# Two heads in one product, quads of heads, and four fixed PSUM areas in a fused attention and expert kernel

## The chip, the cores and the metric

The kernel runs on one core of a Trainium2 chip. The metric is the device time of one execution in microseconds (us); for the kernel before it is the median of three runs. The core has five engines with queues of their own: PE (TensorE, matrix products; its weight loads are shown as PEld), DVE (VectorE), ACT (ScalarE), POOL (GpSimd) and SP (SyncE). PE writes to PSUM; ACT and DVE read PSUM. Each engine takes its instructions in order, and an instruction that waits for another engine holds up all that is queued behind it.

## The reference

Sliding-window causal attention (window 64) over 8 batches, 8 heads, 576 positions and head size 64, then a soft mixture of experts whose slots are fed by a softmax over all 4608 tokens:

```python
scores = scale * np.matmul(q, k.transpose(0, 1, 3, 2))      # q, k, v: 8 x 8 x 576 x 64
rel = pos[:, None] - pos[None, :]
scores = np.where((rel >= 0) & (rel < 64), scores, -1e9)
attn = softmax(scores, axis=-1)
x = np.matmul(attn, v)                                      # then 4608 tokens x 512
logits = x @ phi                                            # 512 x 32 slots
slot_input = softmax(logits, axis=0).T @ x                  # over tokens; 8 experts x 4 slots x 512
slot_out[e] = np.maximum(slot_input[e] @ w1[e], 0) @ w2[e]  # 512 -> 1024 -> 512
out = softmax(logits, axis=1) @ slot_out                    # 4608 x 512
```

## The kernel before

The order of the work is written out by hand. A pair is two heads of one batch: 32 pairs, four to a batch. A loop over n = 0 to 39 (a step) runs a pipeline of stages on different pairs; each step works on one pair in each stage.

- st_transpose(n), L232: 36 transposes of 64x64 on PE bring the pair's queries and keys (tiles qs and ks, loaded as fp16) into a PSUM tile tp with the head size on the partitions. st_copy(n), L235 on ACT, copies them to SBUF, to qkT, one of four.
- st_max(n-1): products of 32 queries by 96 keys on top of a mask, L243 (the mask, 2 x 480 columns) and L250 (36 small products); DVE takes each row's maximum, L253.
- st_shift(n-2): a product L258 turns the maxima round, and DVE copies them, L262, into rt, one of three, from which a product subtracts them before exp.
- st_score(n-3): products with the mask and shift (L270, L274: 8 of 128 columns) and the scores themselves (L278, L283: 64 keys by 64 queries, each head on its half of the partitions). st_exp: exp on ACT, L291 for the last block, L292 for the eight others, into pt.
- st_av(n-4): attention times V, 20 products (L305, L307), with V in two layouts, one shifted by 64 rows by POOL (shift_v, L158 and L159). st_norm on DVE: reciprocal L316 and scaling L317, into x_b.
- fr_transpose(n-5): x_b transposed on PE (L331), copied by ACT (L332) into xt.

Once in a batch, each in a step of its own, come the front stages: logits and their online softmax over tokens (fr_logits at n = 4b+9, L339; fr_exp, L345 to L361), the dispatch transposes (n = 4b+10, L386 to L392) with the softmax over slots (fr_combine, L371 to L382), and the slot sums (n = 4b+11, L399 and L402, accumulated by DVE at L411).

All PSUM tiles of this loop come from one pool of four buffers that go round, whatever the name:

```python
psum = patt.enter_context(tc.tile_pool(name="psum", bufs=4, space=bass.MemoryType.PSUM))
def banks(name):
    t = psum.tile([128, 2, 512], FP32, name=name, tag="ps")
```

Inside a step the stages are called in this order: transposes, scores, copy, exp, attention times V, shift, norm, maxima, logits, x transposes, the rest of the front stages. Loads of q, k and v are made for a whole batch on POOL's queue, the expert weights one tensor every third step; the last expert's weights go into the buffers of q and k after step 32.

After the loop comes the tail, a chain on small data: merging the softmax statistics (L492 to L526), experts 0 to 3 as a group of four in the columns of PE (ha L541, tht L551, op L557), experts 4 to 7 one after the other (hp_ps L570, ReLU on ACT L573, so_ps L578), then the output (cp L595, copies L600 and L602 and the output DMAs).

Of the kernel before, what the change touches and what calls it, by code (L numbers as in the profile page):

```python
# [14 lines left out]
NEG = -60000.0  # L15
# [3 lines left out]
def kernel(  # L19
# [32 lines left out]
    psum = patt.enter_context(tc.tile_pool(name="psum", bufs=4, space=bass.MemoryType.PSUM))  # L52
    pin = ctx.enter_context(tc.tile_pool(name="pin", bufs=2))

    def banks(name):
        t = psum.tile([128, 2, 512], FP32, name=name, tag="ps")
        return t, t[:, :, :].bitcast(FP16)
# [4 lines left out]

    def flat(src, b):
        return src[b].rearrange("h s d -> (h s) d").rearrange("(c p) d -> p c d", p=128)

    def rows(src, b):
        return src[b].rearrange("h s d -> (h s d)").rearrange("(g p x) -> p g x", p=128, x=RQ * Dh)

    staged = {}

    def new_qk(b):
        staged[b] = tuple(pin.tile([128, HP, RQ * Dh], FP16, name=n, tag=n) for n in ("qs", "ks"))

    def load_qk(b, c0=0, c1=HP):
        for t_, src in zip(staged[b], (q, k)):
            nc.gpsimd.dma_start(out=t_[:, c0:c1, :], in_=rows(src, b)[:, c0:c1, :])

    new_qk(0)
    load_qk(0, 0, 1)

    ident_h = const.tile([128, 128], FP16, name="ident_h")
    make_identity(nc, ident_h)
    load_qk(0, 1, HP)
# [22 lines left out]
    def load_last():  # L106
        e = E - 1
        w1_t[e], w2_t[e] = [], []
        for i in range(2):
            a = pin.tile([128, 2, F], FP16, name="w1h", tag="qs")  # L110
            nc.gpsimd.dma_start(out=a, in_=w1_dram(e)[:, 2 * i:2 * i + 2, :])
            w1_t[e].extend(a[:, j, :] for j in range(2))
        for i in range(2):
            c = pin.tile([128, 4, D], FP16, name="w2h", tag="ks")
            for j0, j1 in ((0, 4),) if i == 0 else ((0, 2), (2, 4)):
                nc.gpsimd.dma_start(out=c[:, j0:j1, :], in_=w2_dram(e)[:, 4 * i + j0:4 * i + j1, :])
            w2_t[e].extend(c[:, j, :] for j in range(4))


    wb = const.tile([32, 96], FP16, name="wb")  # L120
    nc.vector.memset(wb, 0.0)
    nc.gpsimd.affine_select(out=wb, in_=wb, compare_op=ALU.is_gt, fill=NEG,
                            base=0, pattern=[[1, 96]], channel_multiplier=-1)
    nc.gpsimd.affine_select(out=wb, in_=wb, compare_op=ALU.is_ge, fill=NEG,
                            base=64, pattern=[[-1, 96]], channel_multiplier=1)

    KR = 75
    mb = const.tile([64, 128], FP16, name="mb")
    nc.vector.memset(mb, 0.0)
    nc.gpsimd.affine_select(out=mb[:, 0:64], in_=mb[:, 0:64], compare_op=ALU.is_gt,  # L130
                            fill=NEG, base=0, pattern=[[1, 64]], channel_multiplier=-1)
    nc.gpsimd.affine_select(out=mb[:, 64:128], in_=mb[:, 64:128], compare_op=ALU.is_ge,
                            fill=NEG, base=0, pattern=[[-1, 64]], channel_multiplier=1)
    db = const.tile([128, 12], FP16, name="db")
    nc.vector.memset(db[64:128, :], 0.0)
    nc.gpsimd.affine_select(out=db[64:KR, 0:10], in_=db[64:KR, 0:10], compare_op=ALU.not_equal, fill=-1.0,
                            base=0, pattern=[[-1, 10]], channel_multiplier=1)
    nc.gpsimd.affine_select(out=db[64:KR, 10:11], in_=db[64:KR, 10:11], compare_op=ALU.not_equal, fill=NEG,
                            base=-10, pattern=[[0, 1]], channel_multiplier=1)
    nc.gpsimd.affine_select(out=db[64:KR, 11:12], in_=db[64:KR, 11:12], compare_op=ALU.not_equal, fill=1.0,  # L140
                            base=-10, pattern=[[0, 1]], channel_multiplier=1)
# [9 lines left out]
    v2s = [pvv.tile([128, NCH, VP], FP16, name=f"v2_{i}") for i in range(2)]  # L151

    def load_v(b):
        nc.gpsimd.dma_start(out=v1s[b % 2][:, :, 0:Dh], in_=flat(v, b))  # L154

    def shift_v(b):
        v1, v2 = v1s[b % 2], v2s[b % 2]
        nc.gpsimd.tensor_copy(out=v2[64:128, :, 0:Dh], in_=v1[0:64, :, 0:Dh])  # L158
        nc.gpsimd.tensor_copy(out=v2[0:64, 1:NCH, 0:Dh], in_=v1[64:128, 0:NCH - 1, 0:Dh])  # L159

    load_v(0)
    new_qk(1)
    load_qk(1)

    NQ = 4
    qkT = [pqk.tile([128, 2, 64 + S], FP16, name=f"qkT{i}") for i in range(NQ)]
    for t_ in qkT:
        nc.vector.memset(t_[:, 1, 0:64], 0.0)
    wm = const.tile([128, 5, 96], FP16, name="wm")
    for t in range(4):  # L170
        nc.vector.tensor_copy(out=wm[32 * t:32 * t + 32],
                              in_=wb[:, :].unsqueeze(1).broadcast_to([32, 5, 96]))
    nc.vector.memset(wm[0:32, 0, 0:64], NEG)
    nc.vector.memset(wm[32:64, 0, 0:32], NEG)

    lh = const.tile([128, 10, 128], FP16, name="lh")
    nc.vector.tensor_copy(out=lh[0:64], in_=mb[:, :].unsqueeze(1).broadcast_to([64, 10, 128]))
    nc.vector.tensor_copy(out=lh[64:128], in_=db[64:128, 0:10].unsqueeze(2).broadcast_to([64, 10, 128]))
    for u in (0, 5):
        nc.vector.tensor_tensor(out=lh[64:128, u, 0:64], in0=lh[64:128, u, 0:64],  # L180
                                in1=db[64:128, 10:11].broadcast_to([64, 64]), op=ALU.add)
    NR = 3
    rts = [const.tile([128, 128], FP16, name=f"rt{i}") for i in range(NR)]
    for rt in rts:
        nc.vector.memset(rt[64:128, 64:128], 0.0)
        nc.vector.tensor_copy(out=rt[64:128, 0:64], in_=db[64:128, 11:12].broadcast_to([64, 64]))
        nc.vector.tensor_copy(out=rt[0:64, 0:64], in_=ident_h[0:64, 0:64])
        nc.vector.tensor_copy(out=rt[0:64, 64:128], in_=ident_h[0:64, 0:64])
# [37 lines left out]
    def st_transpose(p, tq):  # L226
        b, hp = divmod(p, HP)
        for w, src in enumerate(staged[b]):
            for r in range(RQ):
                for hl in range(2):  # L230
                    h = slice(64 * hl, 64 * hl + 64)
                    nc.tensor.transpose(tq[h, w, 64 * r:64 * r + 64], src[h, hp, Dh * r:Dh * r + Dh], ident_h[h, h])  # L232

    def st_copy(p, tq):
        nc.scalar.activation(qkT[p % NQ][:, :, 64:64 + S].rearrange("p w (g r) -> p w g r", r=RQ),  # L235
                             tq[:, :, 0:S].rearrange("p w (r g) -> p w g r", r=RQ), AF.Copy, scale=QKS)

    def st_max(p):
        qk = qkT[p % NQ]
        m = pw.tile([128, 10], FP16, name="m", tag="m")  # L240
        mx, _ = banks("mx")
        for hl in range(2):
            nc.tensor.matmul(mx[:, hl, 0:480], ident_h[:, :], wm[:, :, :].rearrange("p c x -> p (c x)"),  # L243
                             start=True, stop=False, skip_group_check=True)
        for c in range(5):
            for t in range(4 if c < 4 else 2):
# [10 lines left out]
    def st_shift(p, av):  # L257
        nc.tensor.matmul(av[64:74, 1, 384:512], mts.pop(p)[:, :], ident_h[:, :], start=True, stop=True,  # L258
                         skip_group_check=True)
# [380 lines left out]
```

## Time and profile before

| | |
|---|---|
| median of the runs | 270.45 us (269.38 to 273.96, three runs) |
| the profiled execution | 271.76 us, of which the program's span is 270.0 us |
| granted PE clock, mean over the span | 0.799 |
| attention stage: first copy L235 / last copy L235 start | 6.03 / 179.19 us |
| tail: first step of the chain / last copy of the output | 207.2 / 255.5 us |
| HBM read, written | 61.93 MB, 9.44 MB |

In the profile the span is cut into 40 equal slices, in which a digit is the busy share of an engine in tenths; PEclk is the granted share of PE's full clock. A line of a group of instructions gives source line, engine, operation, output<-input, shapes and count, then the busy time of all and the mean ns of one, then the engine's idle time just ahead of them and what ended most of it. A timeline line gives start, duration, engine, line and operation; several equal instructions in a row are merged (x18), with the time from the first's start to the last's end.

### The profile page before, as it was taken

How to read it: one execution, taken by the hardware profiler on the slowest of the kernel's cores; microseconds unless marked ns; L12 is line 12 of the kernel's file. 1: busy time of each engine (PE TensorE's matmuls, PEld its weight loads, DVE VectorE, ACT ScalarE, POOL GpSimd, SP SyncE). 2: the span in 40 equal slices, each digit the busy share in tenths (PEclk: the TensorE clock that was granted, in tenths of full speed). 3: DMA queues.
4: the chain of work that ended last, by engine and by line, in shares of the span. 5: the costliest groups of instructions: out<-in, count | busy, mean ns of one | idle time of the engine just before them, and what ended most of it. 6: DMA issues, size and time to landing. Idle time of an engine off the chain costs nothing. (4 is left out here: it accounts for less than half of the span.)

```text
span 270.0 us, 9905 instructions
## 1 busy us (share of the span) xinstructions
PE 185.6 (69%) x4563; PEld 122.6 (45%) x4563; DVE 140.9 (52%) x313; ACT 120.5 (45%) x215; POOL 78.0 (29%) x74
## 2 busy tenths in 40 slices
PE   2386858858868897887887586878663488866400
PEld 1254646646646665665665365555531134521100
DVE  2743563674754576674485554656664621056510
ACT  2235445655455475574654647462632111155400
POOL 8566064342370533443057033740000000000000
PEclk9998989986985897997799689975955557995555
DMA  6999997992999599199299959899960000029996
GB/s 84 175 206 210 181 208 131 177 207 38 132 211 208 58 187 206 17 177 208 37 100 210 210 73 184 121 203 205 210 105 0 0 4 0 2 101 344 359 359 234
DMA packets 63625, 41.06 MB, mean 152 GB/s; under 512 B 38496, under 2 KB 54880, under 8 KB 63584
## 3 DMA queue, kind: packets, MB, share of 16 engines
q0 software_dynamic: 58064, 30.94, 84.3%
q1 hardware_dynamic: 5520, 9.50, 10.2%
q8 instruction: 35, 0.57, 0.8%
q14 instruction: 6, 0.05, 0.1%
HBM read 61.93 MB, written 9.44 MB: 264 GB/s over the span
## 5 line engine op out<-in xcount | busy, mean ns | idle before, releaser
L235 ACT ACTIVATE qkT<-tp 128x1152 f16<-128x1152 f16 x32 | 36.2, 1131 | 50.2 <-PE tp L278 39.6
L253 DVE TENSOR_REDUCE m<-mx 128x10 f16<-128x960 f32 x32 | 36.8, 1150 | 6.4 <-PE mx L250 6.2
L262 DVE CAST rt<-av 10x128 f16<-10x128 f32 x32 | 9.2, 289 | 51.6 <-PE av L258 50.9
L292 ACT ACTIVATE pt<-sc 128x1024 f16<-128x1024 f32 x32 | 32.9, 1029 | 0.6 <-PE sc L283 0.5
L332 ACT COPY xt<-f 128x576 f16<-128x576 f16 x32 | 20.5, 640 | 26.5 <-PE f L331 26.5
L154 POOL DMA_DIRECT2D v<-in_v_dram x8 | 14.6, 1823 | 55.3 <-issue 35.2
L158 POOL COPY v<-v 64x2304 f16<-64x2304 f16 x8 | 16.8, 2102 | 41.6 <-DMA v<-in_v_dram 41.6
L317 DVE TENSOR_TENSOR x_b<-av,rc 128x640 f16<-128x640 f32 x32 | 26.4, 824 | 1.1
L305 PE MATMUL av<-v,pt 128*64 128x65 f16 x576 | 19.7, 214 | 8.0 <-issue 8.0
L232 PE MATMUL tp<-ident_h,qs 64*64 64x64 f16 x576 | 17.6, 210 | 11.0 <-DMA qs<-in_q_dram 7.9
L274 PE MATMUL sc<-rt,lh 128*128 128x128 f16 x256 | 23.9, 247 | 1.4 <-issue 1.4
L243 PE MATMUL mx<-wm,ident_h 128*128 128x480 f16 x64 | 21.7, 426 | 3.0 <-ACT pt L291 2.7
L305 PEld LDWEIGHTS <-pt 128*64 128x64 f16 x576 | 15.3, 125 | 12.2 <-issue 8.6
L232 PEld LDWEIGHTS <-qs 64*64 64x64 f16 x576 | 14.2, 122 | 14.4 <-DMA qs<-in_q_dram 8.0
L232 PE MATMUL tp<-ident_h,ks 64*64 64x64 f16 x576 | 17.6, 210 | 4.6 <-issue 2.4
L250 PEld LDWEIGHTS <-qkT 64*32 64x32 f16 x1152 | 11.3, 97 | 18.5 <-issue 18.3
L274 PEld LDWEIGHTS <-lh 128*128 128x128 f16 x256 | 18.4, 113 | 1.6 <-issue 1.6
L283 PE MATMUL sc<-qkT 64*128 64x64 f16 x512 | 15.8, 205 | 4.4 <-issue 4.4
L331 PE MATMUL f<-ident_h,x_b 128*128 128x128 f16 x160 | 16.3, 240 | 2.5 <-ACT pt L291 1.2
L250 PE MATMUL mx<-qkT 64*32 64x96 f16 x1152 | 16.2, 221 | 2.2 <-issue 2.2
L232 PEld LDWEIGHTS <-ks 64*64 64x64 f16 x576 | 14.6, 125 | 5.1 <-DMA ks<-in_k_dram 2.6
L159 POOL COPY v<-v 64x2240 f16<-64x2240 f16 x8 | 16.4, 2052 | 0.5
(135 smaller groups left out, 295.0 us busy)
## 6 DMA issues: line engine op xcount, KB each, us to landing
w<-in_moe_w_dram POOLq DMA_DIRECT2D x14, 1024.0 KB, 15.6
out_dram<-ob SPq DMA_DIRECT2D x16, 512.0 KB, 4.5
v<-in_v_dram POOLq DMA_DIRECT2D x8, 576.0 KB, 8.4
qs<-in_q_dram POOLq DMA_DIRECT2D x7, 576.0 KB, 9.6
ks<-in_k_dram POOLq DMA_DIRECT2D x7, 576.0 KB, 11.6
w1h<-in_moe_w_dram POOLq DMA_DIRECT2D x2, 512.0 KB, 18.6
out_dram<-ob SPq DMA_DIRECT2D x8, 128.0 KB, 4.5
w2h<-in_moe_w_dram POOLq DMA_DIRECT2D x1, 512.0 KB, 19.1
```

Of the source, the lines that this page charges most:

```text
L158: nc.gpsimd.tensor_copy(out=v2[64:128, :, 0:Dh], in_=v1[0:64, :, 0:Dh])
L159: nc.gpsimd.tensor_copy(out=v2[0:64, 1:NCH, 0:Dh], in_=v1[64:128, 0:NCH - 1, 0:Dh])
L232: nc.tensor.transpose(tq[h, w, 64 * r:64 * r + 64], src[h, hp, Dh * r:Dh * r + Dh], ident_h[h, h])
L235: nc.scalar.activation(qkT[p % NQ][:, :, 64:64 + S].rearrange("p w (g r) -> p w g r", r=RQ), tq[:, :, 0:S].rearrange("p w (r g) -> p w g r ...
L243: nc.tensor.matmul(mx[:, hl, 0:480], ident_h[:, :], wm[:, :, :].rearrange("p c x -> p (c x)"), start=True, stop=False, skip_group_check=True)
L250: nc.tensor.matmul(mx[32 * t:32 * t + 32, hl, 96 * c:96 * c + 96], qk[r, 0, 64 + o:64 + o + 32], qk[r, 1, o:o + 96], start=False, stop=Tru ...
L253: nc.vector.reduce_max(m[:, :].rearrange("p (l c) -> p l c", l=2), mx[:, :, 0:480].rearrange("p l (c x) -> p l c x", x=96), axis=AXX)
L274: nc.tensor.matmul(sc[:, hl, 128 * c:128 * c + 128], lh[:, 5 * hl + c, :], rt[:, :], start=(c == 0), stop=False, skip_group_check=True)
L292: nc.scalar.activation(pt[:, :, 0:8, :].rearrange("p l i x -> p l (i x)"), sc[:, :, :], AF.Exp, scale=XS)
L305: nc.tensor.matmul(av[r0:r0 + 64, hl, 65 * (i // 2):65 * (i // 2) + 65], pt[:, hl, i, :], rhs, start=True, stop=True, skip_group_check=True)
L317: nc.vector.tensor_tensor(out=xbs[b][:, :, 128 * hp:128 * hp + 128].rearrange("p c (l d) -> p l c d", l=2), in0=avv[:, :, :, 0:64], in1=rc ...
L332: nc.scalar.copy(out=xts[b][:, hp, :], in_=fq[:, 0, 0:S])
```

## The change

- Four fixed PSUM areas a_t, a_v, a_m and a_s, of two banks each, take the place of the pool. a_t takes the transposes of q or k and the last (ninth) block of scores; a_v takes the ninth block of the maxima, the turned maxima and attention times V; a_m takes the other eight blocks of the maxima, and then all of the front stages (x transposes, logits, dispatch, slot sums); a_s takes eight blocks of scores.
- Loads and transposes are by quads: four heads of q or of k, half a batch. An even step transposes a quad's keys, an odd one its queries, 18 transposes each of 128x64. The keys are copied by ACT to kT with two heads on each pair's 128 partitions; the queries by two ACT instructions to qb, in which each block of 128 columns has one head's 64 queries in the upper half of the partitions and the other's in the lower, and zeros elsewhere. A pair is now heads i and i+2 of a quad.
- With that, one product over all 128 partitions gives the scores of two heads: maxima are 9 products of 128x128 on the mask, scores 9 of 128x128 on mask and shift.
- The order in a step is: transposes and their copy, shift and its copy, maxima, attention times V and norm, scores and exp, front stages. The maxima run two steps behind the transposes (one before), the shift three (two before), so only two rt buffers stand.
- x transposes are made for two pairs at once in every second step. fr_exp first copies the logits from PSUM to SBUF on ACT.
- Loads: one DMA for each quad of k, q and v, and the V shift by half batches.
- Tail: experts 0 to 3 and 4 to 6 as two groups in the columns of PE, expert 7 alone as before; so4 is copied by DVE alone.

```diff
-    psum = patt.enter_context(tc.tile_pool(name="psum", bufs=4, space=bass.MemoryType.PSUM))
+    psum = patt.enter_context(tc.tile_pool(name="psum", bufs=1, space=bass.MemoryType.PSUM))
...
+    a_t, a_v, a_m, a_s = [psum.tile([128, 2, 512], FP32, name=n_) for n_ in ("a_t", "a_v", "a_m", "a_s")]
+    a_th, a_mh = a_t[:, :, :].bitcast(FP16), a_m[:, :, :].bitcast(FP16)
...
+    def st_transpose(n, tq):
+        g, odd = divmod(n, 2)
+        src = staged.pop(("qs" if odd else "ks", g))
+        tf = tq.rearrange("p a x -> p (a x)")
+        for r in range(RQ):
+            for hf in range(2):
+                nc.tensor.transpose(tf[64 * hf:64 * hf + 64, 128 * r:128 * r + 128],
+                                    src[:, hf, Dh * r:Dh * r + Dh], ident_h[:, :])
+
+    def st_copy(n, tq):
...
+        if odd:
+            for hf in range(2):
+                h = slice(64 * hf, 64 * hf + 64)
+                nc.scalar.activation(qbs[g % 2][h, :, :, hf, :], tf[h], AF.Copy, scale=QKS)
+        else:
+            nc.scalar.activation(kTs[g % NK][:, :, 64:64 + S], tf, AF.Copy, scale=QKS)
...
     def st_max(p):
...
+        mx = a_m
+        m8 = a_v[:, 0, 384:512]
+        nc.tensor.matmul(m8, ident_h[:, :], wm[:, 1, :], start=True, stop=False, skip_group_check=True)
+        nc.tensor.matmul(m8, qblock(p, 8), kwindow(p, 8), start=False, stop=True, skip_group_check=True)
+        for j in range(2):
+            nc.tensor.matmul(mx[:, j, :], ident_h[:, :], wm[:, j:j + 4, :].rearrange("p c x -> p (c x)"),
                              start=True, stop=False, skip_group_check=True)
...
+        for i in range(8):
+            nc.tensor.matmul(at(mx, m8, i), qblock(p, i), kwindow(p, i), start=False, stop=True,
+                             skip_group_check=True)
+        nc.vector.reduce_max(m[:, 8:9], m8, axis=AXX)
+        nc.vector.reduce_max(m[:, 0:8].rearrange("p (l c) -> p l c", l=2),
+                             mx[:, :, :].rearrange("p l (c x) -> p l c x", x=128), axis=AXX)
...
+    def st_shift(p):
+        t_ = a_v[64:64 + NB, 1, 384:512]
+        nc.tensor.matmul(t_, mts.pop(p)[:, 0:NB], ident_h[:, :], start=True, stop=True, skip_group_check=True)
+        nc.vector.tensor_copy(out=rts[p % NR][64:64 + NB, :], in_=t_)
...
+        sc, sm = a_s, a_t[:, 1, 128:256]
+        for order in (range(8), (8,)):
+            for i in order:
+                nc.tensor.matmul(at(sc, sm, i), lh[:, i, :], rt[:, :], start=(i % 4 == 0), stop=False,
+                                 skip_group_check=True)
+            for i in order:
+                nc.tensor.matmul(at(sc, sm, i), kwindow(p, i), qblock(p, i), start=False, stop=True,
+                                 skip_group_check=True)
+        nc.scalar.activation(pt[:, 0:8, :].rearrange("p i x -> p (i x)"), sc[:, :, :], AF.Exp, scale=XS)
+        nc.scalar.activation(pt[:, 8, :], sm, AF.Exp, scale=XS)
...
     def fr_exp(b, lg):
+        lg_ps, lg = lg, pw.tile([128, 192], FP32, name="lg", tag="lgec")
+        nc.scalar.copy(out=lg, in_=lg_ps)
...
+        f, fq = a_m, a_mh
         if n < NP:
+            st_transpose(n, a_th)
+            st_copy(n, a_th)
         if 0 <= n - 3 < NP:
+            st_shift(n - 3)
+        if 0 <= n - 2 < NP:
+            st_max(n - 2)
         if 0 <= n - 4 < NP:
+            st_av(n - 4, a_v)
+            st_norm(n - 4, a_v)
+        if 0 <= n - 3 < NP:
+            st_score(n - 3)
...
+        xp = n - 6 if n % 2 == 0 and 0 <= n - 6 < NP else None
...
+    groups = ((0, 1, 2, 3), (4, 5, 6))
...
+    for g, es in enumerate(groups):
+        ha, _ = banks("ha")
...
+            if f2 == 0:
+                nc.scalar.activation(hs[g][0:n, 0:512], ha[0:n, 0, :], AF.Relu, scale=emask[0:n, g:g + 1])
+            else:
+                nc.vector.tensor_scalar(out=hs[g][0:n, 512:1024], in0=ha[0:n, 1, :], scalar1=emask[0:n, g:g + 1],
+                                        scalar2=0.0, op0=ALU.mult, op1=ALU.max)
...
-    so4 = ptl.tile([128, D], FP16, name="so4")
-    nc.scalar.copy(out=so4[:, 0:256], in_=so_ps[:, 0:256])
-    nc.vector.tensor_copy(out=so4[:, 256:512], in_=so_ps[:, 256:512])
+    so4 = ptl.tile([128, D], FP16, name="so4")
+    nc.vector.tensor_copy(out=so4, in_=so_ps)
```

The prediction names lines of the new kernel too: L241 its transposes, L250 and L252 the copies of queries and keys, L267 the first product of the maxima's ninth block, L276 the maximum on DVE, L283 DVE's copy of the shift, L296 and L297 the two exps, L339 the x transposes.

## The prediction

> **What bounds the kernel now.** I read the page first, for the engines' shares and the clock.
>
> ```profile
> PE 185.6 (69%) x4563; PEld 122.6 (45%) x4563; DVE 140.9 (52%) x313; ACT 120.5 (45%) x215; POOL 78.0 (29%) x74
> ...
> PE   2386858858868897887887586878663488866400
> ...
> PEclk9998989986985897997799689975955557995555
> ```
>
> ```profile
> L235 ACT ACTIVATE qkT<-tp 128x1152 f16<-128x1152 f16 x32 | 36.2, 1131 | 50.2 <-PE tp L278 39.6
> L253 DVE TENSOR_REDUCE m<-mx 128x10 f16<-128x960 f32 x32 | 36.8, 1150 | 6.4 <-PE mx L250 6.2
> L262 DVE CAST rt<-av 10x128 f16<-10x128 f32 x32 | 9.2, 289 | 51.6 <-PE av L258 50.9
> L292 ACT ACTIVATE pt<-sc 128x1024 f16<-128x1024 f32 x32 | 32.9, 1029 | 0.6 <-PE sc L283 0.5
> ```
>
> PE (TensorE) is at 8 or 9 tenths through the attention stage, and what ACT and DVE wait for is PE (39.6 and 50.9 us). Then the timelines of ACT and of PE around an undisturbed step (columns: start, duration, engine, line):
>
> ```profile
> 115.22 1.13 ACT L235 ACTIVATE qkT<-tp 128x1152 f16<-128x1152 f16 x1 [2.24 <-PE tp L278]
> 116.24 0.27 ACT L291 ACTIVATE pt<-tp 128x128 f16<-128x128 f32 x1
> 116.40 1.03 ACT L292 ACTIVATE pt<-sc 128x1024 f16<-128x1024 f32 x1
> 117.33 0.64 ACT L332 COPY xt<-f 128x576 f16<-128x576 f16 x1
> 119.03 1.13 ACT L235 ACTIVATE qkT<-tp 128x1152 f16<-128x1152 f16 x1 [1.05 <-PE tp L278]
> ```
>
> ```profile
> 117.48 0.47 PE L232 MATMUL tp<-ident_h,qs 64*64 64x64 f16 x18 [0.19 <-ACT pt L292]
> ...
> 118.24 0.61 PE L274 MATMUL sc<-rt,lh 128*128 128x128 f16 x8
> ...
> 119.15 0.34 PE L305 MATMUL av<-v,pt 128*64 128x65 f16 x9
> ...
> 119.58 0.22 PE L258 MATMUL av<-ident_h,m 128*10 128x128 f16 x1
> 119.74 0.58 PE L243 MATMUL mx<-wm,ident_h 128*128 128x480 f16 x2
> 120.25 0.47 PE L250 MATMUL mx<-qkT 64*32 64x96 f16 x36
> ...
> 122.72 0.51 PE L339 MATMUL f<-xt,phi_sb 128*32 128x192 f16 x14 [1.81 <-issue]
> ```
>
> An undisturbed step takes 119.03 - 115.22 = 3.81 us and PE is full in it. Step 4's transposes start at 20.5 us and step 31's at 178 (PE timeline), so the mean step is 157.5 / 27 = 5.83 us. The difference is half clock, the front work of each batch, and stops like the last line's (1.81 us in which PE waits for no one; all such gaps sum to 22 us on PE). The stretches of 3.41 us (length, PE, PEld, DVE, ACT, POOL, granted clock, DMA) show when the clock halves:
>
> ```profile
> 99.83:103.24 3.41, 1.44 (x54) 1.07 (x48) 3.35 (x5) 1.09 (x2) 3.35 (x2) 0.99 1.21 209
> 103.24:106.65 3.41, 3.41 (x64) 2.40 (x58) 1.41 (x6) 2.74 (x8) 0.16 (x1) 0.51 1.14 215
> 106.65:110.07 3.42, 2.69 (x96) 2.03 (x97) 2.54 (x5) 1.97 (x5) 0.00 (x0) 1.00 0.48 91
> 123.72:127.13 3.41, 3.41 (x85) 2.89 (x79) 1.41 (x5) 2.03 (x7) 0.00 (x0) 0.51 1.24 209
> ```
>
> A stretch with PE busy 1.44 of 3.41 is followed by one at half clock; one fully busy brings the clock back. Cut this way over the attention stage, stretches at or below 0.55 busy lost the clock and those at 0.57 or above kept it.
>
> **The change, part by part.** *PE work.* One matmul of 128 columns costs 0.056 us in a row (L274: 8 in 0.61, one alone 0.22), one of 512 0.217 (L578: 8 in 1.90, one 0.38). L305's go to two column halves in turn: from 119.15 to 119.58 is 0.43 for 20 of 65 columns. The new step has 18 transposes of 128 columns in two halves, which the trace lacks: between 18 x 0.028 = 0.50 (halves together, as L305) and 18 x 0.056 = 1.0 (one by one, as L274); I take 0.50, L305 being the same form. Then the maxima: 2 x 0.056 + 2 x 0.217 + 8 x 0.056 = 0.99 (now 0.91 with L243 and L250, 119.74 to L339's 120.65); attention-times-V 0.43, as now; scores 18 x 0.056 = 1.0 (now 0.98, 118.17 to 119.15). So PE work per step only falls from 3.8 to about 3.5. Instructions fall from 9118 to 5534.
>
> *The waits.* Areas with one reader put PE, DVE and ACT in a row. In the new instruction list: the matmul for area a_v's eighth block (L267) waits for DVE's copy of the shift (L283); behind it on PE stand the maxima, V and the scores; the scores are read by exp (L296), then exp of block 8 (L297), and the next step's first transpose (L241) waits for L297, since both are in a_t. Before, four rotating buffers let transposes run beside exp. The loop at full clock: transposes 0.50; shift matmul until DVE starts 0.26 (L258 at 119.58, L262 at 119.84); L262's 0.29; back to PE 0.05; block 8 0.11; maxima 0.88; V 0.43; scores' first 16, 0.84 to the last's start; 0.27 until ACT; exp 1.03 and 0.27, which overlap by 0.1 (L291 and L292), 1.20; back 0.05; three changes of tile shape at about 0.08 (L258 stands 0.12 behind a stream of L307/L305 spaced 0.02 to 0.05), 0.2. Sum 5.1 us against 3.81. ACT's copies lie beside it: keys 1.13 in even steps, queries 2 x 1.13 in odd ones (each half of the partitions has 1152 elements, as L235), xt for two pairs 1.13 every second step (1152 elements, L235's size). In the odd step they end 3.3 us in, the scores at 3.7: hidden, with 0.4 us to spare.
>
> *Front work, once in a batch of four steps.* (a) Logits step: logits, then a new copy of them (128x192, 0.35) behind both exps, DVE's maxima (L345, L346, L348: 0.28 + 0.36 + 0.50 = 1.14), ACT's exps (L355 at 125.67 to L358's end 126.85: 1.18), DVE's sums (0.42), and behind these on DVE's queue the next step's shift copy, for which all PE now waits: it starts 5.05 (exps done) + 0.25 + 1.14 + 0.1 + 1.18 + 0.05 + 0.42 + 0.05 = 8.24 us into the logits step instead of 5.1 + 0.58 + 0.26 = 5.94, +2.3. Now the same row waits too (rt at 127.31) but a step of slack takes it up. (b) Dispatch step: its transposes write a_m and wait until xt is copied, and that copy stands behind both exps; the next transposes stand behind on PE: +1.1. (c) Slots step: acc (0.75) and the last combine operations (L378 to L382: 0.35, 0.19, 0.36, 0.38) stand ahead of the next shift copy: +1.0. So a batch takes 4 x 5.1 + 4.4 = 24.8 us at full clock, against 4 x 5.83 = 23.3 now with everything.
>
> *Clock.* In (a) PE idles about 2.8 us, and in (b) about 1.8: stretches of below 0.55 busy. A drop lasts 3.4 to 7 us and adds about half of PE's share of that, 1.6 to 3 us. One or two drops a batch: 1.6 to 6; I take 3.2.
>
> [...]
>
> *Stops on PE.* 22 us now, over 9118 instructions; by their number 13 us, less where PE waits anyway. 0.3 to 1.6 a batch, I take 0.8.
>
> *Loads.* POOL issues more and smaller loads. From its queue the new step needs V's shift (half-size copies, half of 2.10 and 2.05 us) one step ahead; the batch's loads at the 205 GB/s of the page take 3.2 MB / 205 = 15 us of 28. Nothing, or below the range's width.
>
> *Start.* Step 4 begins when four loads of 288 KB are in (1152 KB is in at 11.6 us now) and one loop has run: about 17.5 instead of 20.5, -3. The constants on DVE cost about the same (12.3 us now).
>
> *Drain.* From step 31 to the tail now 29 us; the new loop is longer, its last steps have no transposes: 0, bounds -4 and +4.
>
> *Tail.* Now 213.44 to 238.73 in the chain of waits, 25.3. New: two groups in ha, 4 x 1.92 and two reads of 0.70 between halves = 9.1; transposes 0.9, ACT's copy of 1024 elements 1.03 and its wait 0.2; op 3.1 and, with the clock back, 1.9; last expert 0.8 + 0.35, so_ps 2.3, so4 0.75. Sum 20.4: -4.9 (bounds -1.5, all at half clock, and -7). The output behind it is bound by its DMA as now.
>
> **Sum.** Batch 24.8 + 3.2 + 0.8 = 28.8, step 7.2. (7.2 - 5.83) x 27 = +37; -3 - 4.9 gives +29. The profiled execution has a span of 270.0 and 271.76 us in all, 1.3 over the median of 270.45: on the median 270.45 + 29 = 300.
>
> **Rivals.** [...] 0.15.
> *PE alone decides* (faster): if L267 and L241 find their readers done, what counts is PE's work, 0.3 less a step (-10), the stops 40% less (-9), start and tail (-8): 243. For it: PE is what others wait for now. It decides only if the loop's non-PE terms (0.26 + 0.34 + 0.27 + 1.25 = 2.1 us) find other PE work, and the list has none behind those waits. 0.08.
> *The transposes' halves run one by one*: 0.5 more in each loop, more at half clock: +13 to +20, 313 to 320. Against: L305. 0.13.
> *ACT becomes the bound*: copies 6 x 1.13, exps 4 x 1.20, xt 2 x 1.13 and 2.5 of front work are 16.3 us a batch; below the loop even undisturbed, so no case of its own.
>
> **Numbers.** Forecast 0.62 at 300, its own bounds (clock 1.6 to 6, stops, drain, tail) 282 to 318; 0.02 for what I don't see. The range 272 to 322 takes in the first and most of the third rival. 2% is 5.4 us and about what a measurement can tell. Faster: the second rival and a shred, 0.09. Same (265 to 276): the first, 0.14. Slower 0.77.
>
> **What would show it.** Right: L241 waits for ACT L297 in nearly every step, L267 for DVE L283; DVE's L283 late once a batch; PE busy down to about 60% and clock 0.7 to 0.8; undisturbed steps about 5.1 us. Wrong: undisturbed steps at 4 us, or L241 waiting for nothing; transposes of about 1 us; a clock of 0.95.

## The result, and the profile after

The changed kernel takes 311.98 us (median of four runs, 310.7 to 313.48) against 272.2 us of the kernel before in runs beside it (269.38 to 274.83): a ratio of 1.156 [1.146, 1.166]. The profiled execution took 313.48 us, with a span of 311.7 us and a mean granted clock of 0.787, against 270.0 and 0.799. So 41.7 us of span are to be explained; the prediction's sum was 29. Executions of one kernel differ by some per cent, with the granted clock (beside e10 the kernel before took 268.97 us at 0.814 and 279.19 at 0.751): the medians here are of all of them, the ratios of the faster ones alone.

The page of the changed kernel, first the busy shares and the slices of PE and of its granted clock, then four groups (the last columns are the idle time just ahead of the group, and what ended most of it):

```profile
PE 192.3 (62%) x2771; PEld 142.2 (46%) x2771; DVE 152.9 (49%) x340; ACT 138.7 (44%) x219; POOL 96.1 (31%) x113
...
PE   1666117846776675777577767776674743796510
...
PEclk9999758995897979899757967797959555697555
...
L296 ACT ACTIVATE pt<-a_s 128x1024 f16<-128x1024 f32 x32 | 32.7, 1023 | 95.9 <-PE a_s L294 95.9
...
L283 DVE CAST rt<-a_v 9x128 f16<-9x128 f32 x32 | 9.2, 289 | 38.6 <-PE a_v L282 38.2
L267 PE MATMUL a_v<-wm,ident_h 128*128 128x128 f16 x32 | 7.4, 231 | 31.9 <-DVE rt L283 31.9
...
L313 PE MATMUL a_v<-v,pt 128*64 128x65 f16 x64 | 13.3, 216 | 15.4 <-DMA v<-in_v_dram 15.4
```

PE stands mostly at 6 or 7 tenths where it stood mostly at 8. It now waits in the middle of its own list: L267 for DVE's copy of the shift 31.9 us, L241 for ACT's L297 another 15.9 us (the line below, from the view of all waits: us in all, times, longest), and L313, a product of attention times V, 15.4 us for a DMA. In turn DVE's copy waits for PE, and ACT's exp (L296) waits 95.9 us for the scores, where it had waited 0.6. Nobody is busy all the time: the engines wait for each other in a ring.

```profile
PE a_t L241 <- ACT pt L297: 15.9, 21, 1.2
```

The wait for V is one place above all. PE's timeline in step 6 (start, duration, engine, line; in brackets the idle time and what ended it):

```profile
32.50 0.34 PE L311 MATMUL a_v<-v,pt 128*64 128x65 f16 x9
45.49 0.22 PE L313 MATMUL a_v<-v,pt 128*64 128x65 f16 x1 [12.64 <-DMA v<-in_v_dram]
```

and POOL's timeline at the same time:

```profile
30.52 1.22 POOL L153 DMA_DIRECT2D v<-in_v_dram  x1
```

The reader is to see a load that is issued in the step that waits for it (30.52, the step's transposes start at 30.20) and that PE needs at 32.8. It lands 14.9 us after its issue, among 3.1 MB that move at about 200 GB/s in these 16 us. It loads the first half of batch 2, while this step multiplies with the second half of batch 0, which lies in the same buffer; why PE waits for it all the same is the subject of the first experiment.

The ordinary loop is seen in the stretch of PE's timeline that holds one batch:

```profile
121.17 0.69 PE L241 MATMUL a_t<-ident_h,ks 128*64 128x128 f16 x18 [0.79 <-ACT pt L297]
124.61 0.26 PE L267 MATMUL a_v<-wm,ident_h 128*128 128x128 f16 x1 [2.60 <-DVE rt L283]
130.77 0.22 PE L397 MATMUL a_m<-ident_h,d 128*128 128x128 f16 x1 [1.62 <-ACT xt L341]
132.27 0.22 PE L267 MATMUL a_v<-wm,ident_h 128*128 128x128 f16 x1 [0.38 <-DVE rt L283]
136.14 0.69 PE L241 MATMUL a_t<-ident_h,ks 128*64 128x128 f16 x18 [0.52 <-ACT pt L297]
138.07 0.22 PE L267 MATMUL a_v<-wm,ident_h 128*128 128x128 f16 x1 [1.08 <-DVE rt L283]
142.00 0.69 PE L241 MATMUL a_t<-ident_h,qs 128*64 128x128 f16 x18 [0.67 <-ACT pt L297]
143.22 0.22 PE L267 MATMUL a_v<-wm,ident_h 128*128 128x128 f16 x1 [0.38 <-DVE rt L283]
147.15 0.69 PE L241 MATMUL a_t<-ident_h,ks 128*64 128x128 f16 x18 [0.78 <-ACT pt L297]
```

The undisturbed step is the last one, 147.15 - 142.00 = 5.15 us, with its two waits of 0.67 and 0.38. The step that begins at 121.17 stands behind the logits: it holds 2.60 us of wait for DVE, and with the next transposes at 131.05 it takes 9.88 us, 3.4 of them at half clock. In it lies the dispatch's wait for xt (1.62). The step from 136.14 holds 1.08 us of wait behind the slots' work and takes 5.86.

### The profile page after: what moved, and what is told of

Same layout as the page of the kernel before. It is cut to its first block, busy times and chain, and to the rows that moved or that the text cites. A ratio compares the mean times of both kernels' runs of the same rounds, so it can differ in the third digit from the quotient of the medians.

```text
span 311.7 us, 6463 instructions
## 1 busy us (share of the span) xinstructions
PE 192.3 (62%) x2771; PEld 142.2 (46%) x2771; DVE 152.9 (49%) x340; ACT 138.7 (44%) x219; POOL 96.1 (31%) x113
## 4 chain that ended last, share of the span: by engine, by line
PE 44%; DVE 16%; DMA 15%; ACT 11%; issue 9%; POOL 1%; DVEq 0%; ACTq 0%; POOLq 0%
DMA v<-in_v_dram 10%; PE a_s L291 6%; PE a_m L273 5%; PE a_m L270 5%; PE a_s L294 5%; PE a_t L241 4%; PE a_v L311 4%; DMA out_dram<-ob 3%; ACT xt L341 3%; DVE rt L283 3%; PE a_m L339 2%; PE ha L546 2%; PE a_v L267 2%; DVE m L276 2%; DMA qs<-in_q_dram 2%
## 5 line engine op out<-in xcount | busy, mean ns | idle before, releaser
L296 ACT ACTIVATE pt<-a_s 128x1024 f16<-128x1024 f32 x32 | 32.7, 1023 | 95.9 <-PE a_s L294 95.9
L276 DVE TENSOR_REDUCE m<-a_m 128x8 f16<-128x1024 f32 x32 | 39.2, 1224 | 29.6 <-PE a_m L273 29.6
L250 ACT ACTIVATE qb<-a_t 64x1152 f16<-64x1152 f16 x32 | 36.1, 1127 | 5.2 <-PE a_t L241 4.9
L153 POOL DMA_DIRECT2D v<-in_v_dram x16 | 19.6, 1224 | 39.4 <-PE a_v L313 21.9
L73 POOL DMA_DIRECT2D qs<-in_q_dram x16 | 11.4, 712 | 56.0 <-PE a_v L282 55.2
L283 DVE CAST rt<-a_v 9x128 f16<-9x128 f32 x32 | 9.2, 289 | 38.6 <-PE a_v L282 38.2
L267 PE MATMUL a_v<-wm,ident_h 128*128 128x128 f16 x32 | 7.4, 231 | 31.9 <-DVE rt L283 31.9
L311 PEld LDWEIGHTS <-pt 128*64 128x64 f16 x576 | 16.0, 130 | 24.1 <-issue 17.9
L324 DVE TENSOR_TENSOR x_b<-a_v,rc 128x640 f16<-128x640 f32 x32 | 26.4, 824 | 1.1
L273 PEld LDWEIGHTS <-qb 128*128 128x128 f16 x256 | 21.7, 117 | 11.0 <-issue 6.0
L273 PE MATMUL a_m<-kT,qb 128*128 128x128 f16 x256 | 24.8, 254 | 0.0
L291 PE MATMUL a_s<-rt,lh 128*128 128x128 f16 x256 | 24.7, 254 | 0.0
L270 PE MATMUL a_m<-wm,ident_h 128*128 128x512 f16 x64 | 24.0, 463 | 0.4 <-ACT xt L341 0.4
L241 PE MATMUL a_t<-ident_h,ks 128*64 128x128 f16 x288 | 12.1, 232 | 18.6 <-ACT pt L297 10.7
L252 ACT ACTIVATE kT<-a_t 128x1152 f16<-128x1152 f16 x16 | 18.0, 1123 | 12.2 <-PE a_t L241 12.2
L294 PE MATMUL a_s<-qb,kT 128*128 128x128 f16 x256 | 23.3, 244 | 0.0
L294 PEld LDWEIGHTS <-kT 128*128 128x128 f16 x288 | 22.8, 112 | 0.0
L313 PE MATMUL a_v<-v,pt 128*64 128x65 f16 x64 | 13.3, 216 | 15.4 <-DMA v<-in_v_dram 15.4
L291 PEld LDWEIGHTS <-lh 128*128 128x128 f16 x288 | 21.9, 114 | 1.7
L311 PE MATMUL a_v<-v,pt 128*64 128x65 f16 x576 | 20.3, 219 | 3.5 <-DVE rt L283 3.5
L241 PEld LDWEIGHTS <-ks 128*64 128x64 f16 x288 | 10.9, 116 | 20.6 <-issue 14.2
## 6 DMA issues: line engine op xcount, KB each, us to landing
w1h<-in_moe_w_dram POOLq DMA_DIRECT2D x4, 256.0 KB, 20.6
```

Source lines behind the costliest of these rows:

```text
L153: nc.gpsimd.dma_start(out=v1s[b % 2][:, c, 0:Dh], in_=v[b].rearrange("h s d -> (h s) d").rearrange("(c p) d -> p c d", p=128)[:, c, :])
L241: nc.tensor.transpose(tf[64 * hf:64 * hf + 64, 128 * r:128 * r + 128], src[:, hf, Dh * r:Dh * r + Dh], ident_h[:, :])
L250: nc.scalar.activation(qbs[g % 2][h, :, :, hf, :], tf[h], AF.Copy, scale=QKS)
L270: nc.tensor.matmul(mx[:, j, :], ident_h[:, :], wm[:, j:j + 4, :].rearrange("p c x -> p (c x)"), start=True, stop=False, skip_group_check=True)
L273: nc.tensor.matmul(at(mx, m8, i), qblock(p, i), kwindow(p, i), start=False, stop=True, skip_group_check=True)
L276: nc.vector.reduce_max(m[:, 0:8].rearrange("p (l c) -> p l c", l=2), mx[:, :, :].rearrange("p l (c x) -> p l c x", x=128), axis=AXX)
```

## The experiments

All kernels but e7 are the changed kernel with edits, from the second on with that of e1 in them; e7 is the kernel before with one part of the change. The table is read from PE's timeline of each profiled execution: the start of the transposes of steps 4 and 31 (front of the loop, 27 steps), the time from step 31 to the first product of the tail (drain), and the stretch from the first product of ha to the first of cp (tail). Half clock is the time within these 27 steps in which the granted clock was 0.5 (in the changed kernel, cut into stretches of 3.41 us from 18.33 on, it is 1.00 or 0.50 in each); with the mean granted clock g of the 27 steps it is 2 x (1 - g) x length, as far as the rounding of g goes. e1 and e8 were measured a second time, as e10 and e11, and stand in the table as these. The profiled execution of e4 is the slowest of its four, that of e11 the fastest of its six.

| kernel | span | step 4 | mean step | half clock, us | drain | tail |
|---|---|---|---|---|---|---|
| before | 270.0 | 20.5 | 5.81 | 41 | 30.0 | 25.3 |
| after | 311.7 | 19.9 | 7.39 | 68 | 38.8 | 17.3 |
| e10 own half of V | 294.9 | 21.9 | 6.65 | 37 | 36.7 | 20.7 |
| e11 wait filled | 283.2 | 20.2 | 6.22 | 7 | 38.5 | 20.7 |
| e2 ninth exp first | 291.2 | 19.4 | 6.59 | 37 | 37.1 | 20.5 |
| e3 maxima ahead of the ninth | 278.5 | 20.6 | 6.15 | 14 | 35.5 | 20.5 |
| e4 scores ahead of V (on e3) | 263.7 | 20.0 | 5.66 | 14 | 33.6 | 20.6 |
| e5 sums behind the shift | 274.3 | 21.7 | 6.00 | 10 | 34.2 | 20.4 |
| e6 all of these | 254.0 | 19.2 | 5.39 | 10 | 32.1 | 20.7 |
| e9 front work in the shadow | 237.7 | 19.1 | 4.91 | 0 | 32.8 | 17.3 |
| e7 before, new tail | 264.5 | 21.2 | 5.90 | 51 | 28.2 | 18.6 |

**The wait for V.** st_av fills the rows beside the last block with a product on the first chunk of V's buffer, for both halves of a batch; nobody reads these rows. In odd quads that chunk belongs to the other half, which the load issued in the same step, ahead of the product, overwrites for the batch after next. The edit takes the first chunk of the quad's own half:

```diff
-            nc.tensor.matmul(av[64:128, hf, 260:325], pt[:, 8, 64 * hf:64 * hf + 64], v1[:, 0, 0:65],
+            nc.tensor.matmul(av[64:128, hf, 260:325], pt[:, 8, 64 * hf:64 * hf + 64], v1[:, NVC * gq, 0:65],
```

> The changed kernel, but the filler product L313 (its rows are never used) reads a chunk of V of the quad's own half batch in place of chunk 0, which for every second quad waits for a load two batches ahead, issued in that very step. Theory (a false wait on V's load, 12.6 + 1.7 + 1.1 us on PE): these waits vanish, L313 waits for no DMA, and the time falls from 312 by 13 to 16 us to 296 to 299. Rival (the loads as such are late, DMA or POOL's queue being the bound): the wait moves to the next user of a load (L241 or L311) and the time stays at 308 or above.

Measured: 295.93 us (294.75 to 300.64) beside 273.51 of before, ratio 1.086 [1.075, 1.097]; so some 16 to 19 us less than the changed kernel (by the times and by the ratios), where the waits stand at 15.4 us; in e1 L313 waits for no DMA any more. The mean step falls from 7.39 to 6.65 (in e10, the same kernel again), and that is (7.39 - 6.65) x 27 = 20 us: the loop lost some clock with the wait, too. The half clock falls from 68 to 37 us, and part of that was the wait itself. The rest of the loss stays.

**The clock.** The wait behind the logits is filled with work that nobody reads: eight products of 512 columns, in six of the steps, into a_s, which the scores overwrite. Kernel e1 with this (PE does more, nothing of the result hangs on it):

```diff
             st_shift(n - 3)
+        if n % 4 == 2 and 10 <= n < NP + 2:
+            for i in range(8):
+                nc.tensor.matmul(a_s[:, i % 2, :], ident_h[:, :], wm[:, 0:4, :].rearrange("p c x -> p (c x)"),
+                                 start=True, stop=True, skip_group_check=True)
```

> e1 with more work: in one step of each batch, the one behind the logits, eight products of 512 columns into a_s, whose values are overwritten unread, stand between the shift product and L267, where PE waits for DVE's shift copy; 1.7 us of PE at full clock, 3.4 at half. Theory (the waits cost twice, the second time because the clock halves after them, which makes 44 us at half clock between steps 4 and 31 in e1): the half clock falls to 15 to 30 us and the time by 4 to 10 us against e1, to 286 to 292, though 14 us of work are added. Rival (the clock does not follow from this wait, or its half does not cost): the same as e1 or up to 8 us more.

Measured: 289.41 us (286.76 to 292.19), ratio 1.068 [1.033, 1.103] beside 274.85, too wide to set against e1, which was measured on another chip. So both were measured again, on one chip:

> e1 once more, on the same chip as the next run, so that the two can be compared directly: 294 to 298 us, 40 to 48 us at half clock between steps 4 and 31.

> e8 once more beside e1. Theory: 4 to 9 us less than e10, with 15 to 30 us at half clock. Rival (the difference of e1 and e8 lay between the chips of two calls): within 2 us of e10.

Measured: e10, which is e1, 296.57 us (293.47 to 297.56), 1.094 [1.088, 1.100]; e11, which is e8, 288.17 us (284.97 to 290.97), 1.056 [1.048, 1.064]. The kernel that does more work is 8.4 us faster, and the intervals are apart. The stretches from step 4 to step 31 (length, PE, PEld, DVE, ACT, POOL, granted clock, DMA), e10 first:

```profile
21.90:201.40 179.50, 126.38 (x2126) 102.55 (x2125) 100.89 (x222) 100.52 (x158) 72.28 (x76) 0.90 1.08 141
```

```profile
20.20:188.10 167.90, 124.31 (x2174) 96.17 (x2173) 101.22 (x222) 100.55 (x158) 73.41 (x77) 0.98 1.14 149
```

PE carries out 48 products more (2174 against 2126), is busy 2 us less, and runs at 0.98 of its clock instead of 0.90. The added products can't shorten any chain of work, so what the kernel gains comes from the clock: 8.4 us by the medians, and 11.6 us in this stretch of the two profiled executions, of which e11's is its fastest. The half clock fell from 37 to 7 us, further than the 15 to 30 expected (and e10's 37 lies below its 40 to 48). The same view gives, for the changed kernel and for the kernel before,

```profile
19.90:219.50 199.60, 132.90 (x2128) 107.28 (x2129) 100.88 (x222) 100.95 (x158) 73.65 (x78) 0.83 0.99 129
```

```profile
20.50:177.30 156.80, 121.44 (x3588) 88.38 (x3584) 93.53 (x195) 86.82 (x154) 61.16 (x47) 0.87 1.14 152
```

**The ring, one link at a time.** First link: the next transposes wait for the exp of the ninth block, which stands behind the exp of the other eight. Its turn is changed (on top of e1):

```diff
-        nc.scalar.activation(pt[:, 0:8, :].rearrange("p i x -> p (i x)"), sc[:, :, :], AF.Exp, scale=XS)
         nc.scalar.activation(pt[:, 8, :], sm, AF.Exp, scale=XS)
+        nc.scalar.activation(pt[:, 0:8, :].rearrange("p i x -> p (i x)"), sc[:, :, :], AF.Exp, scale=XS)
```

> e1, and exp of the ninth block (L297, which frees a_t) stands ahead of exp of the eight others (L296). Theory (the serial loop: the next transposes wait for the last reader of a_t): an undisturbed step falls from 5.15 to about 4.4 us and the time by 15 to 25 us against e1, to 273 to 283. Rival (the half clock and PE's own work set the time, the wait on L297 is a symptom): within 4 us of e1.

Measured: 294.15 us (291.08 to 299.37), 1.078 [1.064, 1.091]. That is within the noise of e1, and the expected 15 to 25 us did not come. Undisturbed steps fell from 5.15 to between 4.3 and 4.9 us, but the time did not: the mean step is 6.59 against 6.65. The wait of L267 in this kernel (engine, line, what for; us in all, times, longest), and in e10:

```profile
PE a_v L267 <- DVE rt L283: 43.4, 31, 4.2
```

```profile
PE a_v L267 <- DVE rt L283: 32.0, 31, 3.1
```

The 15.6 us that L241 waited for L297 in e10 are gone, and 11.4 of them are back at L267. The step behind the logits became longer (11.8 and 12.4 us in two batches, against 9.7 to 10.6 in e10): its end hangs on the chain of logits, DVE's maxima, ACT's exps and DVE's sums, which does not start earlier because the transposes do. So what one link gives is taken back by the next. A second cause adds to it: one operation of that chain, L359, took 0.8 to 1.1 us instead of 0.16 in four batches (one in e10), beside copies by POOL (see the last section); that is about 2.7 us more than in e10, in all. DVE's and PE's timelines of this kernel show such a step:

```profile
133.19 1.12 DVE L359 TENSOR_TENSOR nmax<-nmax,nb 128x1 f32<-128x1 f32 x1
...
136.12 0.29 DVE L283 CAST rt<-a_v 9x128 f16<-9x128 f32 x1
```

```profile
136.46 0.27 PE L267 MATMUL a_v<-wm,ident_h 128*128 128x128 f16 x1 [4.21 <-DVE rt L283]
```

L283 stands behind the sums on DVE's queue, and L267 waits for it 4.21 us; 1.12 of the chain ahead of it are L359.

Second link: the ninth block of the maxima writes a_v, so it waits for the shift's reader, and the eight others, which write a_m, stand behind it. The two products go behind them (on top of e1):

```diff
-        nc.tensor.matmul(m8, ident_h[:, :], wm[:, 1, :], start=True, stop=False, skip_group_check=True)
-        nc.tensor.matmul(m8, qblock(p, 8), kwindow(p, 8), start=False, stop=True, skip_group_check=True)
         for j in range(2):
...
+        nc.tensor.matmul(m8, ident_h[:, :], wm[:, 1, :], start=True, stop=False, skip_group_check=True)
+        nc.tensor.matmul(m8, qblock(p, 8), kwindow(p, 8), start=False, stop=True, skip_group_check=True)
         nc.vector.reduce_max(m[:, 8:9], m8, axis=AXX)
```

> e1, and the eight maxima products in a_m (L270, L273) stand ahead of the ninth block's in a_v (L267, L268), so that they run while DVE copies the shift. Theory: L267's wait of 0.38 us a step goes, but attention times V then stands right behind the ninth block and waits 0.5 us for DVE to read it (L275); only the step behind the logits gains some 0.9 us. Net within 6 us of e1. Rival (L267's 32 us of waiting are the whole loss): 20 us or more less than e1.

Measured: 280.39 us (277.08 to 280.72), 1.027 [1.014, 1.040], 15.5 us below e1 beside it, where at most 6 were expected. The waits of this kernel for DVE (the ninth block's first product is L273 here):

```profile
PE a_v L273 <- DVE rt L283: 12.3, 9, 2.1
PE a_v L311 <- DVE m L275: 11.6, 30, 0.5
```

Together they are 8 us less than L267's 32.0 in e10. The rest goes with the clock: the half-clock time of the loop fell from 37 us to 14. In four of the stretches of 3.41 us behind the logits PE is now busy 0.54, and the clock holds; in e10 such stretches are busy 0.25 to 0.29 and lose it, as five do in the changed kernel at 0.24 to 0.28.

Third link: the scores ahead of attention times V, so that ACT's exp starts while PE still has V to do (on top of e3):

```diff
+        if 0 <= n - 3 < NP:
+            st_score(n - 3)
         if 0 <= n - 4 < NP:
             st_av(n - 4, a_v)
             st_norm(n - 4, a_v)
-        if 0 <= n - 3 < NP:
-            st_score(n - 3)
```

> e3, and the scores with their exps stand ahead of attention times V in the step. Theory: the loop loses the wait for the shift copy (0.38) and the 0.43 us of attention times V, which then run under exp: an undisturbed step of about 4.35 us, time 20 to 30 us less than e1, 267 to 277. Rival (half clock and PE work): within 5 us of e1.

Measured: 264.72 us (260.77 to 265.5), 0.965 [0.949, 0.980]; some 31 us below e1, against 20 to 30 expected; with it the changed loop is at last faster than the one before (5.66 us a step against 5.81).

Fourth link: DVE's two sums of the statistics, ahead of the next step's shift copy on DVE's queue, go behind it (on top of e1; "stats" holds the two additions, and "later" is a list that is worked off there):

```diff
-        nc.vector.scalar_tensor_tensor(out=stat[:, 1:2], in0=stat[:, 1:2], scalar=al[:, :], in1=s2[:, 0:1],
-                                       op0=ALU.mult, op1=ALU.add)
-        nc.vector.tensor_tensor(out=stat[96:128, 1:2], in0=stat[96:128, 1:2], in1=s2[96:128, 1:2], op=ALU.add)
+        later.append(stats)
...
             st_shift(n - 3)
+        while later:
+            later.pop(0)()
```

> e1, and DVE's two sums of the online softmax (L370, L372), which wait for ACT's exps, are queued behind the next step's shift copy (L283) instead of ahead of it. Theory (DVE's queue holds the shift copy, and PE waits for it once a batch): L283 comes 1.2 to 1.6 us earlier in the step behind the logits, L267's longest wait falls from 3.1 to about 1.5 us, the time falls by 10 to 16 us against e1, to 280 to 286. Rival (ACT's queue holds that step: the keys' copy stands behind the same exps): within 4 us of e1.

Measured: 276.68 us (275.62 to 277.4), 1.020 [1.012, 1.027], 18 to 19 us below e1 (measured on another chip; by the ratios and by the times), where 10 to 16 were expected. The two additions are 0.22 and 0.16 us long, but they waited for ACT's exps: L267's longest wait fell from 3.1 to 2.1 us and its sum from 32.0 to 22.2, and the half clock from 37 us to 10.

```profile
PE a_v L267 <- DVE rt L283: 22.2, 31, 2.1
```

Nine to ten of the 18 to 19 us are the waits themselves.

**Together.** e6 has all four, and the slots' last combine operations (L389 to L393) behind the next shift copy too:

```diff
-            pending.pop(sb)()
+            later.append(pending.pop(sb))
```

> e4 with the exp of the ninth block first (e2), the sums (e5) and the combine operations (L389 to L393) behind the next step's shift copy. Theory (serial waits, each hidden now by other work, and with them the half clock): undisturbed steps at 4.0 to 4.4 us, the step behind the logits at 6 to 6.5, time 248 to 257, less than both kernels. Rival (what e2 showed: a wait taken away is given back at the next one): 260 or above, as e4.

Measured: 256.38 us (255.63 to 258.02), 0.947 [0.938, 0.956].

**The front work in the shadow.** e9 goes on: fr_exp but for its first copy is issued behind the next step's shift copy on every engine, its sums behind that step's norm, and the copy of xt on ACT, which the dispatch's transposes had to wait for, is issued behind them (all of the computation is kept):

```diff
-            fr_exp(lb, lg)
+            later.append(fr_exp(lb, lg))
...
+        while sums:
+            sums.pop(0)()
...
         if db_ is not None:
             fr_dispatch(db_, fq)
+        if xp is not None:
+            fr_transpose_copy(xp, fq)
+        if db_ is not None:
             fr_dispatch_copy(db_, fq)
```

> e6, and the online softmax of the logits behind the next step's keys' copy and shift copy (all but the copy of the logits), its sums behind that step's norm, and ACT's copy of xt behind the dispatch transposes on PE. Theory (what is left of the front work in the loop is the queue ahead of L283 and the dispatch's wait for xt): the step behind the logits falls from 7.1 to 5 to 5.5 us, time 236 to 248. Rival (PE's work decides by now, or the exps in front of the scores' exps hold ACT): 253 or more.

Measured: 240.43 us (238.72 to 242.14), 0.892 [0.872, 0.911] of the kernel before. Its page, and the wait of its first exp, the ninth block's (L296 here; the eight others' exp follows it without a wait on the scores of its own):

```profile
PE 166.5 (70%) x2771; PEld 121.4 (51%) x2771; DVE 152.4 (64%) x340; ACT 137.6 (58%) x219; POOL 96.1 (40%) x113
...
PE   0398978988878697788878868877744387877300
...
PEclk9999999999999999999999999997965558975555
```

```profile
ACT pt L296 <- PE a_t L294: 27.0, 25, 3.9
```

The same products on the same four areas: PE has 7 to 9 tenths again and its full clock through the whole loop, the step behind the logits takes 4.84 us where it took 9.88, and ACT's 95.9 us of waiting for the scores have become 27.0. The mean step, 4.91, is 0.9 below the one of the kernel before. What each of the parts that e9 adds to e6 is worth was not tried.

**The tail by itself.** The kernel before, with only the new tail (experts 4 to 6 as a second group in PE's columns, so4 copied by DVE):

```diff
+    groups = ((0, 1, 2, 3), (4, 5, 6))
...
+    for g, es in enumerate(groups):
+        ha, _ = banks("ha")
...
+                for j, e in enumerate(es):
+                    nc.tensor.matmul(ha[32 * j:32 * j + 32, f2, :], sit[:, kk, :],
+                                     w1_t[e][kk][:, 512 * f2:512 * f2 + 512],
+                                     start=(kk == 0), stop=(kk == NKK - 1), skip_group_check=True)
...
-    for e in range(4, E):
+    e = E - 1
...
-    nc.scalar.copy(out=so4[:, 0:256], in_=so_ps[:, 0:256])
-    nc.vector.tensor_copy(out=so4[:, 256:512], in_=so_ps[:, 256:512])
+    nc.vector.tensor_copy(out=so4, in_=so_ps)
```

> The kernel before with the tail of the changed one alone (experts in groups of four and three, expert 7 alone). Theory (the tail's 25 us chain falls to 17): 7 to 9 us less than the kernel before. Rival (the shorter tail came from the clock that the changed attention stage left): within 3 us of it.

Measured: 265.5 us (264.73 to 266.26), 0.979 [0.972, 0.986]: about 6 to 7 us, a little less than the 7 to 9 expected, the stretch from ha to cp being 18.6 instead of 25.3. The granted clock in that stretch was 0.71 against 0.75 before, so the gain is not one of the clock. That part of the change was a gain.

## Why the prediction was right, and where its sum was wrong

The terms of the forecast against the profiled spans, with e10 (the changed kernel without the false wait) beside it:

| term | forecast | after | e10 |
|---|---|---|---|
| 27 steps | +37 | 199.6 - 156.8 = +42.8 | 179.5 - 156.8 = +22.7 |
| start (step 4) | -3 | -0.6 | +1.4 |
| drain | 0 | +8.8 | +6.7 |
| tail | -4.9 | -8.0 | -4.6 |
| rest | 0 | -1.3 | -1.3 |
| span | +29 | +41.7 | +24.9 |

The direction and the mechanism were right: engines that wait for each other, and a clock that falls with them (0.83 over the 27 steps, where it was 0.87). That the sum came so near is in part luck. Without the false wait the loop costs 22.7 us and not 37, so the sum had 14 us too much there; the false wait put 20 back on the loop, the drain and the start another 11, and the tail took 3 off.

*The step that failed: "Loads. ... Nothing, or below the range's width."* I asked whether POOL could issue the loads in time and whether their bytes fit, not what each reader of V's buffer reads. A product whose result nobody uses read a chunk under rewriting, and 12.64 + 1.65 + 1.07 = 15.4 us of PE came of it; e1 took some 16 us off, more than all of the difference between 312 and the forecast's 300. The instruction list would have shown it: L313 waits there for a load's queue.

*The loop.* Right, link by link. The undisturbed step was put at 5.1 us and is 5.15; L241 waits for L297, though in 21 steps and not in nearly every one, and L267 for L283 in 31. L241's 18 transposes take 0.69 us, which is the 0.50 that was reckoned to the last one's start and the length of that one (a single product of this size stands at 0.22). The mean step before was put at 5.83, with step 31 at 178; its transposes start at 177.3, so it is 5.81.

*Front work.* (a) said +2.3 behind the logits; L267 waits 2.60 instead of 0.38, +2.2. Its term of 0.50 for L348 was a mean: the trace before has 0.16 six times, and 1.36 and 1.72 beside copies by POOL. (b) said +1.1; the wait for xt is 1.62 in the step shown and 1.2 to 1.6 in the others within the loop. (c) said +1.0; the step is 5.86 - 5.15 = +0.7. Together 4.4 was forecast. The batch at full clock was put at 24.8 us: e11, at 0.98 of the clock and with the added products in the wait, takes 4 x 6.22 = 24.9.

*Clock.* The cause was right, its size too large: 3.2 us a batch, against 4 x (6.65 - 6.22) = 1.7 in e10. In the changed kernel the batch is 4 x 7.39 = 29.6, of which 15.4 / 6.75 batches = 2.3 is V's wait and 24.9 the full-clock part: 2.4 is left for the clock. e3 and e5, where small edits gained 15.5 and 19 us, show how steep it is: in the loop of the changed kernel every stretch of 3.41 us is granted the whole clock or half of it, 1.00 or 0.50; behind a stretch at the whole clock in which PE is busy 0.44 or less the next one is at half, behind one of 0.60 and more it is not, so a little work more or less can decide over all of it. Over the 27 steps the granted clock is 0.83 here with four areas passed round, and 1.00 in e9 with the same areas and fewer waits.

*Stops on PE.* 0.8 us a batch was forecast; 22 us of such gaps stood before, and after the change no matmul's gap is ended by "issue", so this term of the sum is nothing. Why they went was not tried; the instruction queue fetched 0.34 MB in 21 packets where it had fetched 0.57 MB in 35.

*Start.* -3 was forecast, -0.6 came: the first transposes wait 5.48 us, and step 2 for ACT's copy of the queries. *Drain.* 0 (bounds -4 and +4) was forecast, +8.8 came. The maxima, the shift and the x transposes come one step later than before, in a loop of as many steps, and in the last steps nothing hides the front work: L267 waits 2.75 us and later L311 3.50 us for DVE's L283. In e9, without such waits, the drain is still 32.8, so some 3 us are left; what they go to was not tried. *Tail.* -4.9 was forecast with the clock partly back, -4.6 came in e10 at a granted clock of 0.63, and -8.0 in the changed kernel at 0.81, past the bound of -7 that I had given for full clock.

*The rivals.* The first, that the clock holds, is out: it was granted at 0.83 over the steps. "PE alone decides" is out for this kernel, by 47.8 us of waits at L267 and L241; but its 243 us were named with the condition that other work of PE is put behind those waits, and e9, which does so, takes 240. That the two figures lie so close is not shown to be more than chance: PE still waits in e9. "The halves one by one" gave 313 to 320, which is near the time, and is still out: the 18 transposes take 0.69 us, not over 1.0. The time alone would have picked the wrong cause. ACT as the bound is out: 44% busy, waiting for the scores.

One expectation behind the prediction failed as well: e2 was to bring 15 to 25 us and brought about 2, since I had priced the link of the undisturbed step for all steps; the step behind the logits ends by another chain and took it back. e3 and e5 were the reverse: priced as waits, without the clock that they gave back.

## What to carry to other kernels

When buffers that go round become fixed areas with one reader at a time, draw the ring (PE, reader, PE) for the plain step and for each step with extra work, and order every queue so that behind each such wait there is work that does not hang on it: the same change was worth 1.156 or 0.892, by the order of the queues and one false read. Ask of every read of a reused buffer, those whose result is thrown away above all, which load may be writing it. And price a wait by the clock, too: in e5, with the longest waits shorter by 1 us, the loop had 27 us less of half clock.

## What the runs showed of the hardware

- A DVE operation of one element per partition can take a microsecond. L359 (nmax) takes 0.16 us; in e2 it took 0.79 to 1.12 us in four of its eight executions, and these four are the ones beside POOL's copies of V (L160, 1.14 us from 133.15 on, in the step shown; L162 in one). In the changed kernel L359 took 0.90 us beside a copy, and L391, 0.36 us alone, took 0.85 and 1.05 beside one, but the short sums of L372, 0.15 to 0.16 us beside a copy too, were not held up. In the four cases in the changed kernel L372 had started 0.01 us before the copy, while L359 and L391, where they were slow, started 0.20 to 0.50 us behind the start of one and ended with it or 0.2 us behind it. What holds them up was not shown.
- Adding work to an engine can make a kernel faster: 48 products more, 8.4 us less (e11 against e10).
- In the changed kernel the clock was lost behind some stretches of 3.41 us with PE busy 0.53 to 0.58 (0.53 from 195.83 on, 0.58 from 107.08), and kept behind others at 0.53 to 0.57 (0.53 from 100.25 on, 0.57 from 62.71); so the bound that I read from the kernel before, between 0.55 and 0.57, is not sharp. It came back also behind stretches of 0.86 to 0.95, not only full ones; behind one of 0.89, from 158.28 on, it did not.
- Transposes on PE counted for the clock. In e9 the stretch from 67.90 has PE busy 2.29 of 3.41 us; without its 30 transposes some 0.8 us are left, 0.24 of the stretch, and the clock stays at 1.00. In the kernel before the stretch from 55.40 is busy 1.48 us, 0.43 of it, with no transpose in it, and the next one has a clock of 0.50.
